# Unread TensorE products, one merged copy and a new split of work between ScalarE, GpSimd and VectorE in the first quarter of a fused attention and feed-forward kernel

## The chip, the cores and the metric

One core of a Trainium2 chip runs the kernel. Times are device microseconds (us) from the first to the last instruction of one execution, and a profile shows one execution with every engine's instructions. The engines are TensorE (PE: matmuls; PEld: its weight loads), VectorE (DVE), ScalarE (ACT), GpSimd (POOL) and SyncE (SP), which issues the transfers. Each takes its own instructions strictly in the order in which they stand in its queue.

## The reference

Attention with an additive bias that a small network makes of positions, and then two feed-forward layers over the 2304 tokens (B = 4 batches, H = 8 heads, S = 576 positions, D = 64, all float32):

```
scores = q @ k.T / sqrt(64) + bias            # bias[h,i,j] = sum_m max(x[i,j]*w1[m]+b1[m], 0) * w2[m,h]
x[i,j] = log1p(|i-j|) / log1p(max(i,1))
attn   = exp(scores - max); attn /= sum(attn) + 1e-9;  y = attn @ v
y      = (silu(y @ w_gate) * (y @ w_val)) @ w_out          # 512 -> 1536 -> 512
out    = relu(y @ w_in)**2 @ w_out2                        # 512 -> 2048 -> 512
```

The feed-forward weights come as float64, and VectorE decodes them from their bits.

## The kernel before

**Arithmetic.** Nearly every float32 product is made of three float16 ones: an operand is split into a high part and the rest (the low part), and high x high, high x low and low x high are added up. `halves` does such a split in one of several ways: 1 takes the scaled high part on GpSimd (L197) and the low part on VectorE (L191); 0 takes the high part on ScalarE (L201) and the low part on VectorE; 2 scales the whole operand in place on ScalarE (L205), rounds it there (L209), and takes the low part on GpSimd (L220). The table `MIX` gives for each kind of operand the ways that its calls take in turn; `mixed` picks the next.

**Stages.** Attention goes by query tiles of 128 rows: tile 0, 1, 2, 3 and a merged tile of the last 64 rows of each batch. Before each tile, `make_bias` makes its bias for all heads in 18 blocks of 32 keys: VectorE makes a mask (L595), TensorE multiplies it (L633), and `evac` takes the sums out of PSUM into the bias. Way 2 of `evac` has ScalarE copy both sums (L609, L615) and GpSimd multiply and add (L610, L616); way 0 has VectorE do both in two instructions that read PSUM (L612 and L618 of the changed file).

**Tile 0.** The 32 pairs of batch and head (heads, below) go one after the other. For a head, TensorE makes the scores (`scores`, L801), VectorE adds the bias and finds the maximum (L810), ScalarE takes the exponential with the row sums (L815). One head later `soft2` has TensorE transpose the float32 weights in five pieces into PSUM (L834, L835) and ScalarE copy them out (L836, L837), and `weighted` multiplies them with the values in float32 (`av`, L850). The fifth piece holds the last 64 keys. In the later tiles the weights are split into float16 halves and turned by transfers. While tile 0 runs, `prep_k` splits and transposes the keys of four heads at a time (eight groups, each with a large chunk of 512 positions and a small one of 64; the transposes are L699), and the stream of weights goes on: w_gate and w_val in thirds of 512 columns (a transfer, three decode instructions on VectorE L256 to L261, a square on ScalarE L318, a norm on TensorE L322, the split), then w_out (key "o"), whose 12 pieces are split when the scale of the whole matrix is known (L169 spreads it over the partitions).

**Feed-forward.** `moe1` takes units of 256 tokens: 24 products for each of 12 blocks (L453), a tanh on ScalarE (L461), two VectorE operations, a split, then 72 products with w_out (L476). The second layer comes at the end (L1353 and L1385).

**Order.** The program is written as generators that are taken in turn by declared costs, and a scheduler then sets the order in each engine's queue from priorities and modelled times. A change of an instruction's engine or size so moves others too. Of the 1283 us, attention and the first layer hold about the first 900, and tile 0 with its bias the first 245.

## Time and profile before

| | |
|---|---|
| median of 3 runs | 1277.08 us (1276.87 to 1277.08) |
| the profiled execution | 1284.85 us, its span 1283.2 us |
| busy: PE, DVE, ACT, POOL | 89%, 61%, 55%, 51% of the span |
| mean granted TensorE clock | 0.954 of full speed |

The share of TensorE is that of an engine that bounds most of the program. "Granted clock" is the part of TensorE's full speed that it was allowed to run at: 1.00 is 2.4 GHz and 0.50 is 1.2 GHz, and a mean between them says how long each was granted. A busy TensorE at 0.50 gets half as much done.

### The profile page before, as it was taken

To read this page: it belongs to the slowest core of one execution; us is meant where nothing else is said; L and a number is where in the kernel's file an instruction comes from. 1 tells how busy PE (TensorE), PEld (TensorE's weight loads), DVE (VectorE), ACT (ScalarE), POOL (GpSimd) and SP (SyncE) were. 2 spreads that over 40 slices of the span, in tenths; PEclk is the share of its full clock that TensorE was granted. 3 is DMA by queue.
4 is the path that set the end of the run, shared out by engine and by line. 5 is a ranking of instruction groups with operands and counts; after the bars stand their busy time and mean duration, and the time that the engine had idled before them with its cause. 6 is when DMAs were issued, how large, how long until landed. Compare 5 with 4: busy or idle time off the path is not lost.

```text
span 1283.2 us, 27543 instructions
## 1 busy us (share of the span) xinstructions
PE 1138.1 (89%) x10648; PEld 841.9 (66%) x10648; DVE 788.1 (61%) x1828; ACT 705.5 (55%) x1478; POOL 660.3 (51%) x756
## 2 busy tenths in 40 slices
PE   2568989998868999999899997989987999999998
PEld 2456768777557768687685764757436567485687
DVE  5787756788768665566573534987677352623523
ACT  5667767767657555556665432437753452715433
POOL 1851103379858666758676440324796350714423
PEclk9998678999969999999999998899999999999999
DMA  9747544127999989999789994572001010010000
GB/s 233 196 131 184 168 129 109 32 82 165 218 212 214 228 190 185 198 207 172 183 173 213 236 228 125 189 229 67 17 1 34 33 34 34 1 50 17 17 34 17
DMA packets 290110, 166.35 MB, mean 130 GB/s; under 512 B 245308, under 2 KB 258620, under 8 KB 289980
## 3 DMA queue, kind: packets, MB, share of 16 engines
q1 hardware_dynamic: 289980, 164.61, 54.9%
q8 instruction: 83, 1.36, 0.4%
q14 instruction: 47, 0.39, 0.1%
HBM read 91.60 MB, written 19.48 MB: 87 GB/s over the span
## 4 chain that ended last, share of the span: by engine, by line
PE 44%; DMA 20%; DVE 15%; POOL 8%; ACT 7%; issue 5%; SPq 1%; POOLq 0%; ACTq 0%; DVEq 0%
PE mm L1353 11%; PE mm L1385 10%; PE mm L453 8%; DMA pT<-pt 7%; PE mm L476 4%; DMA qT<-qs 3%; PE av L850 2%; POOL pt L220 2%; PE av L860 2%; DMA wr<-in_moe_w_gate_dram 2%; PE qk L801 2%; PE ma L1385 2%; POOL bias L616 2%; POOL btmp L610 2%; DMA w2s<-in_moe_w_in_dram 2%
## 5 line engine op out<-in xcount | busy, mean ns | idle before, releaser
L453 PE MATMUL mm<-xT,wr 128*128 128x256 f16 x2376 | 294.9, 281 | 11.7 <-DVE th L464 9.1
L453 PEld LDWEIGHTS <-wr 128*128 128x128 f16 x2592 | 255.3, 101 | 63.7 <-issue 21.2
L1165 POOL TENSOR_TENSOR x<-x 128x256 f32<-128x256 f32 (+1 forms) x160 | 143.5, 908 | 174.1 <-ACT x L1362 168.0
L1353 PE MATMUL mm<-wr,w2r 128*128 128x512 f16 (+1 forms) x960 | 189.9, 360 | 6.3 <-ACT x L1358 6.3
L220 POOL TENSOR_TENSOR pt<-s,pt 128x576 f16<-128x576 f32 x112 | 147.1, 1317 | 35.5 <-ACT pt L825 29.2
L1353 PEld LDWEIGHTS <-w2r 128*128 128x128 f16 x960 | 94.3, 98 | 99.2 <-issue 8.6
L220 POOL TENSOR_TENSOR z<-th,z 128x256 f16<-128x256 f32 x108 | 82.6, 765 | 138.0 <-ACT z L438 132.9
L810 DVE CUSTOM_DVE_ANT_0 s<-qk,bias 128x576 f32<-128x576 f32 x144 | 107.7, 751 | 52.6 <-PE qk L801 31.3
L476 PE MATMUL mm<-wr,z 128*128 128x512 f16 x576 | 136.0, 382 | 1.0 <-DVE th L464 1.0
L818 ACT ACTIVATE s<-s,sc 128x576 f32<-128x576 f32 x112 | 85.7, 772 | 71.5 <-DVE sc L817 63.0
L1385 PEld LDWEIGHTS <-wr 128*128 128x128 f16 x1134 | 110.6, 98 | 21.2 <-DVE wr L1165 5.6
L610 POOL TENSOR_TENSOR btmp<-btmp,xs 128x256 f32<-128x256 f32 (+1 forms) x108 | 88.2, 819 | 67.9 <-ACT btmp L609 44.3
L1165 DVE TENSOR_TENSOR wr<-x,wr 128x768 f16<-128x768 f32 (+3 forms) x60 | 78.0, 1310 | 65.6 <-ACT wr L1172 64.6
L860 PE MATMUL av<-vp,pT 128*128 128x65 f16 (+7 forms) x1920 | 87.0, 197 | 28.5 <-DMA pT<-pt 26.1
L595 DVE TENSOR_TENSOR mask<-tabT,bias 128x1024 f16<-128x1024 f16 (+1 forms) x108 | 91.7, 867 | 22.5 <-PE ma L633 16.4
L476 PEld LDWEIGHTS <-z 128*128 128x128 f16 x648 | 60.3, 98 | 66.3 <-issue 2.5
L860 PEld LDWEIGHTS <-pT 128*128 128x128 f16 (+3 forms) x1920 | 72.3, 102 | 47.7 <-DMA pT<-pt 34.4
L616 POOL TENSOR_TENSOR bias<-bias,btmp 128x256 f32<-128x256 f32 (+1 forms) x108 | 77.3, 719 | 6.1 <-DVE vp L191 0.7
L633 PEld LDWEIGHTS <-mask 128*128 128x128 f16 x1440 | 60.7, 106 | 29.9 <-issue 15.6
L1404 ACT ACTIVATE ob<-ob,fac 128x256 f32<-128x256 f32 x36 | 17.8, 506 | 105.4 <-DVE ob L1403 105.4
L462 DVE SCALAR_TENSOR_TENSOR th<-th,mm 128x256 f32<-128x256 f32 x99 | 41.0, 414 | 47.3 <-ACT th L461 45.2
L438 ACT CAST z<-th 128x256 f16<-128x256 f32 x108 | 43.0, 399 | 44.4 <-DVE th L464 43.8
(269 smaller groups left out, 2117.1 us busy)
## 6 DMA issues: line engine op xcount, KB each, us to landing
kp<-kT_d SPq DMA_DIRECT2D x64, 288.0 KB, 3.4
vp<-v_d SPq DMA_DIRECT2D x48, 325.0 KB, 4.1
w2s<-in_moe_w_in_dram SPq DMA_DIRECT2D x16, 512.0 KB, 4.2
w2s<-in_moe_w_out_dram SPq DMA_DIRECT2D x16, 512.0 KB, 4.4
wr<-in_moe_w_gate_dram SPq DMA_DIRECT2D x24, 256.0 KB, 5.0
wst<-in_moe_w_out_dram SPq DMA_DIRECT2D x12, 512.0 KB, 4.3
wr<-in_moe_w_val_dram SPq DMA_DIRECT2D x24, 256.0 KB, 4.9
v_d<-vp SPq DMA_DIRECT2D x16, 325.0 KB, 3.1
```

Of the source, the lines that this page charges most:

```text
L220: nc.gpsimd.tensor_tensor(out=out_, in0=x, in1=hi, op=ALU.subtract)
L453: nc.tensor.matmul(pg[:, 256 * gi:256 * gi + 256], wr.parts(key, f // 4, cc, wl, P * (f % 4), P), mov(xl, cc), start=k == 0, stop=k == 11)
L476: nc.tensor.matmul(po, zall[:, f, zl, P * t:P * t + P], wr.parts("o", 0, f, wl), start=k == 0, stop=k == 3 * NF1 - 1)
L595: nc.vector.tensor_tensor(out=m[:, :, ni * e:ni * e + ni], in0=block(kb, i0, ni), in1=th, op=ALU.is_gt)
L610: nc.gpsimd.tensor_tensor(out=tmp[r], in0=tmp[r], in1=xb, op=ALU.mult)
L616: nc.gpsimd.tensor_tensor(out=bias[r, :, cs], in0=bias[r, :, cs], in1=tmp[r], op=ALU.add)
L810: nc.vector.tensor_tensor_reduce(out=s.rearrange("p (a j) -> p a j", a=2), in0=pq[:, :, 0:288], in1=bias[:, n].rearrange("p (a j) -> p a j ...
L818: nc.scalar.activation(s, s, AF.Exp, bias=nm, scale=-1.0)
L860: nc.tensor.matmul(av[r, slot, 0:cn], pT[:n, 5 * l + c, r], vs[e][c][:n, c0:c0 + cn], start=m == 0, stop=m == 14)
L1165: (nc.gpsimd if how else nc.vector).tensor_tensor(out=out_, in0=a, in1=b, op=op)
L1353: nc.tensor.matmul(ph[:, :n], w2r.parts("w", g // 4, cc, wl, P * (g % 4), P), yt[:, 4 * yl + cc, :], start=m == 0, stop=m == 11)
L1385: nc.tensor.matmul(po, HS[f][:, o:o + P], st["C7"][f][wl][:, b:b + 256], start=f == 0 and k == 0, stop=f == 7 and k == 2)
```

## The change

It has five parts. (1) In tile 0, `soft2` puts four products of 128 x 512 ahead of a head's transposes; they write to the PSUM room that the transposes then overwrite, so nobody reads them. They are there as long as fewer than 14 heads have been multiplied with the values, which gives 15 heads and 60 products. (2) The fifth transpose takes the last 128 keys rather than the last 64, the values of the last 64 keys are loaded to partitions 64 to 127, and one copy of 640 columns takes the place of two. (3) `prep_k` takes way 1 for both chunks (high part on GpSimd, low part on VectorE). (4) The bias of tiles 0 and 1 takes way 2 and way 0 in turn, 9 blocks each. (5) w_out is split by way 2 (two steps on ScalarE, the rest on GpSimd) in place of way 0.

```diff
-    "g": (1, 2), "v": (1,), "o": (0,), "w": (0, 1, 2), "2": (1, 2), "K": (0, 2),
-    "V": (0,), "b": (2,), "B": (2,), "h": (0,), "H": (0, 1), "x": (0, 0, 1),
+    "g": (1, 2), "v": (1,), "o": (2,), "w": (0, 1, 2), "2": (1, 2), "K": (1,),
+    "V": (0,), "b": (2, 0), "B": (2,), "h": (0,), "H": (0, 1), "x": (0, 0, 1),
...
-                how = mixed("b" if t == 0 else "B")
+                how = mixed("b" if t in (0, 1) else "B")
...
-    def soft2(s, pt):
+    def soft2(s, pt, warm=None):
...
+            if warm is not None and av_done[0] < 14:
+
+                for _ in range(4):
+                    nc.tensor.matmul(
+                        tr[:, 0, :], ident_h, warm[:, 0:4, :], start=True, stop=True)
...
-            nc.tensor.transpose(tr[0:64, 1, 0:P], s[:, 512:S], ident)
-            nc.scalar.copy(pf[:, 0:512], tr[:, 0, :])
-            nc.scalar.copy(pf[0:64, 512:640], tr[0:64, 1, 0:P])
+
+            nc.tensor.transpose(tr[:, 1, 0:P], s[:, S - P:S], ident)
+            nc.scalar.copy(pf, tr.rearrange("p a j -> p (a j)")[:, 0:640])
...
-                n = P if c < 4 else 64
+                r = slice(0 if c < 4 else 64, P)
...
-                pT = soft2(*pend_soft[2:])
+                pT = soft2(*pend_soft[2:], st.get(("q", pend_soft[0], 0, pend_soft[1] // 4)))
```

Lines after 830 carry numbers higher by 5 to 6 in the changed file (the scores stay L801, the four transposes become L839, the fifth L841, the copy L842, the products with the values L855; the unread products are L836).

TensorE's queue about the eleventh head of tile 0, before (a name ahead of the arrow is what is written):

```order
L801 MATMUL qk<-kva,qT 128x288
L131 MATMUL mm<-ident,sc 1x128
L834 MATMUL tr<-ident,s 128x128 x4
L835 MATMUL tr<-ident,s 64x128
L850 MATMUL av<-kva,pT 128x64 x4
L801 LDWEIGHTS qT
```

and the same place in the changed kernel:

```order
L801 MATMUL qk<-kva,qT 128x288
L131 MATMUL mm<-ident,sc 1x128
L836 LDWEIGHTS ident_h
L836 MATMUL tr<-qT,ident_h 128x512
...
L855 MATMUL av<-kva,pT 128x64 x5
L801 LDWEIGHTS qT
L801 MATMUL qk<-kvb,qT 128x288
...
L839 MATMUL tr<-ident,s 128x128 x4
L841 MATMUL tr<-ident,s 128x128
```

The transposes, which wait for the exponential, have moved behind the unread products, the products with the values of an earlier head and the next head's scores.

VectorE's queue in the bias of tile 0, at its middle, before:

```order
L595 TENSOR_TENSOR mask<-tabT,bias 128x1024 x3
L256 TENSOR_SCALAR wr<-wr 128x512
L595 TENSOR_TENSOR mask<-tabT,bias 128x1024
L259 SCALAR_TENSOR_TENSOR wr<-wr 128x512
L595 TENSOR_TENSOR mask<-tabT,bias 128x1024
```

and in the changed kernel:

```order
L595 TENSOR_TENSOR mask<-tabT,bias 128x1024
L618 SCALAR_TENSOR_TENSOR bias<-qk_274,keep_207,btmp 128x8x32
L595 TENSOR_TENSOR mask<-tabT,bias 128x1024
L612 SCALAR_TENSOR_TENSOR btmp<-qk_320,keep_207,xs 128x256
L618 SCALAR_TENSOR_TENSOR bias<-qk_320,keep_207,btmp 128x8x32
L595 TENSOR_TENSOR mask<-tabT,bias 128x1024
L256 TENSOR_SCALAR wr<-wr 128x512
```

Every other block's two VectorE instructions now stand between the masks, ahead of the decodes.

ScalarE's queue at the end of tile 0, where the scale of w_out becomes known (keep_2439), in the changed kernel; before, single pieces of w_out (L201) stood here between tanh and copies:

```order
L815 ACTIVATE s,sc<-s,sc 128x576
L842 COPY pT<-tr 128x640
L735 ACTIVATE qs<-qf 128x4x2x64
L205 ACTIVATE wr<-wr,keep_2439 128x512 x12
L209 CAST wr<-wr 128x512
L461 ACTIVATE th<-mm,ux 128x256
L842 COPY pT<-tr 128x640
```

All 12 scalings stand in one block, ahead of a unit's tanh and of a head's copy. TensorE's queue there has, behind the product that spreads the scale (L169): 24 products of a unit, five transposes, 24 more products, and then the products with the values that need that copy:

```order
L169 MATMUL mm<-sc,ones_r 128x2
L453 LDWEIGHTS wr
L453 MATMUL mm<-xT,wr 128x256
...
L839 MATMUL tr<-ident,s 128x128 x4
L841 MATMUL tr<-ident,s 128x128
...
L855 MATMUL av<-kvb,pT 128x64 x5
L633 LDWEIGHTS mask
```

The products with the values (L855), which stood between the two runs of 24 before, come behind both.

## Rows read from the trace of the kernel before

**Rows 1.** Stretches: start:end, length, busy PE PEld DVE ACT POOL, clock, DMA share, GB/s
```profile
40.00:80.00 40.00, 19.72 (x251) 16.41 (x248) 32.52 (x55) 22.86 (x50) 33.24 (x33) 1.00 0.60 150
80.00:112.00 32.00, 28.69 (x234) 23.52 (x235) 27.23 (x67) 24.55 (x57) 5.02 (x6) 0.95 0.68 173
112.00:120.00 8.00, 4.82 (x29) 4.12 (x29) 4.80 (x13) 7.88 (x20) 2.23 (x2) 0.77 0.81 169
120.00:140.00 20.00, 19.16 (x91) 15.57 (x90) 16.82 (x38) 10.58 (x26) 4.73 (x4) 0.50 0.53 138
140.00:155.00 15.00, 14.02 (x84) 11.93 (x84) 10.72 (x24) 10.11 (x24) 2.76 (x3) 0.65 0.57 172
155.00:185.00 30.00, 24.22 (x160) 19.85 (x160) 14.05 (x41) 21.31 (x54) 0.66 (x1) 0.77 0.57 165
...
205.00:217.00 12.00, 11.39 (x79) 9.00 (x79) 9.44 (x26) 8.31 (x21) 4.42 (x5) 0.72 0.34 99
...
245.00:300.00 55.00, 50.91 (x627) 38.10 (x625) 42.47 (x93) 34.65 (x83) 42.26 (x50) 1.00 0.26 69
```

**Rows 2.** TensorE in order of time about 115 us: start, us, instruction, [idle before]
```profile
112.69 0.66 PE L834 MATMUL tr<-ident,s 128*128 128x128 f32 x4
...
113.98 0.27 PE L131 MATMUL mm<-ident,sc 128*1 128x128 f32 x1
117.39 1.09 PE L834 MATMUL tr<-ident,s 128*128 128x128 f32 x4 [3.13 <-DVE sc L810]
...
118.48 1.81 PE L850 MATMUL av<-kva,pT 128*128 128x64 f32 x8
```

**Rows 3.** Chain of work that ended last, 112 to 156 us: start, us, what
```profile
111.69 8.30 DMA wr<-in_moe_w_val_dram
```

**Rows 4.** The same chain over the first 82 us, shares by line
```profile
by line: DMA wr<-in_moe_w_gate_dram 24.2%; DMA wr<-in_k_dram 14.4%; issue 10.7%; POOL btmp L610 9.2%; POOL bias L616 6.8%; DMA wr<-in_v_dram 6.5%; DVE wr L256 4.5%; DVE wr L259 4.4%; DVE kvb L191 3.8%; DVE wr L261 2.9%; DVE mask L595 2.4%; 
```

**Rows 5.** Instructions of the bias of tile 0: count, ns minimum/median/maximum
```profile
L610 POOL TENSOR_TENSOR btmp<-btmp,xs x18: 716/726/5767, 22.6 to 74.5; 128x256 f32<-128x256 f32 x18
...
L616 POOL TENSOR_TENSOR bias<-bias,btmp x18: 709/784/1237, 23.5 to 75.8; 128x256 f32<-128x256 f32 x18
```

**Rows 6.** A VectorE operation of 128 x 256 that reads PSUM (line L462)
```profile
L462 DVE SCALAR_TENSOR_TENSOR th<-th,mm x18: 398/417/422, 186.5 to 296.5; 128x256 f32<-128x256 f32 x18
```

**Rows 7.** The chain in the last layer: products of 512 float16 columns
```profile
1004.43 41.44 PE mm L1353 x192
```

**Rows 8.** High part of the keys on ScalarE; a high part on GpSimd (lines L201, L197)
```profile
L201 ACT ACTIVATE kvb<-wr x7: 1041/1061/1077, 29.1 to 186.7; 128x1024 f16<-128x1024 f32 x7
...
L197 POOL TENSOR_SCALAR wr<-wr,keep x18: 695/838/1584, 64.1 to 223.4; 128x512 f16<-128x512 f32 x18
```

**Rows 9.** The two copies of tile 0 (lines L836, L837)
```profile
L836 ACT COPY pT<-tr x32: 562/572/592, 83.5 to 235.9; 128x512 f32<-128x512 f32 x32
...
L837 ACT COPY pT<-tr x32: 243/258/285, 84.0 to 237.1; 64x128 f32<-64x128 f32 x32
```

**Rows 10.** GpSimd's waits, 80 to 245 us: in total, times, longest
```profile
POOL wr L197 <- DVE keep L291: 10.4, 2, 7.9
```

**Rows 11.** The split of w_out, 232 to 262 us; GpSimd's low part (L220) earlier
```profile
L201 ACT ACTIVATE wr<-wr,keep x12: 710/722/723, 234.9 to 257.1; 128x512 f16<-128x512 f32 x12
...
L191 DVE SCALAR_TENSOR_TENSOR wr<-wr,keep x12: 740/752/1210, 235.7 to 258.2; 128x512 f16<-128x512 f32 x12
...
L220 POOL TENSOR_TENSOR wr<-wr x6: 1153/1156/1534, 69.5 to 212.7; 128x512 f16<-128x512 f32 x6
```

**Rows 12.** TensorE in order of time where w_out's scale is spread
```profile
232.15 0.38 PE L169 MATMUL mm<-sc,ones_r 1*128 1x2 f32 x2
232.46 2.79 PE L453 MATMUL mm<-xT,wr 128*128 128x256 f16 x24
...
235.81 2.78 PE L453 MATMUL mm<-xT,wr 128*128 128x256 f16 x24
```

**Rows 13.** ScalarE in order of time: two scalings in a row; first piece of w_out
```profile
62.22 1.35 ACT L205 ACTIVATE wr<-wr,keep 128x512 f32<-128x512 f32 x2
...
234.93 0.72 ACT L201 ACTIVATE wr<-wr,keep 128x512 f16<-128x512 f32 x1 [0.62 <-DVE keep L187]
```

More of the change, by code (lines that the diff above doesn't have):

```diff
@@ L650, in load_kv @@
         nc.sync.dma_start(
-            f[0:64, 1024:1280].rearrange("p (h d) -> p h d", h=4),
+            f[64 * which:64 * which + 64, 1024:1280].rearrange("p (h d) -> p h d", h=4),
             src[b, hs, 512:S, :].rearrange("h p d -> p h d"))
@@ L660, in norm_v @@
         nc.scalar.activation(
-            junk[0:64, 0:256], f[0:64, 1024:1280], AF.Square, accum_out=vss[0:64, 8 + h:9 + h])
+            junk[64:P, 0:256], f[64:P, 1024:1280], AF.Square, accum_out=vss[64:P, 8 + h:9 + h])
         x = f.rearrange("p (c d) -> p c d", d=D)
@@ L848, in weighted @@
             for c in range(5):
-                n = P if c < 4 else 64
+                r = slice(0 if c < 4 else 64, P)
                 nc.tensor.matmul(
-                    av[:, slot, 0:64], pT[:n, c, :], vs[0][c][:n], start=c == 0, stop=c == 4)
+                    av[:, slot, 0:64], pT[r, c, :], vs[0][c][r], start=c == 0, stop=c == 4)
             return
```

## The prediction, written before the result

> **What bounds the kernel now.** I cut the span into stretches first and read busy time and granted clock of each [rows 1]. Everything that the change touches lies before 300 us. From 80 to 155 us TensorE is busy for 28.69 + 4.82 + 19.16 + 14.02 = 66.7 of 75 us, so it is the bound of tile 0, yet at a clock that sinks to 0.50 (1.2 GHz). What the low clock costs in a stretch is about its busy time times one minus the clock: 1.4 us (80 to 112), 1.1 (112 to 120), 9.6 (120 to 140), 4.9 (140 to 155), 5.6 (155 to 185), 3.2 (205 to 217), 25.8 in all. Then I looked at how it begins: in order of time TensorE waits for 3.13 us at 114 us, and the four transposes that took 0.66 us take 1.09 after it [rows 2]. The chain of waits shows what was late: a transfer of w_val that lands at 120 us [rows 3], for which VectorE's decode waits ahead of a head's scores. In the stretch before, at 0.95, the same mix of scores, transposes and value products ran fast, so it can be held at the high clock, but it did not regain it by 140 us.
>
> Ahead of tile 0, from 40 to 80 us, GpSimd is busy 33.2 of 40 us and VectorE 32.5 [rows 1]. The chain over the first 82 us has GpSimd's two bias instructions with 9.2 + 6.8 = 16.0%, 13.1 us [rows 4]. After 300 us the change moves nothing by itself; the relative places of attention and feed-forward in TensorE's queue come together again there, so a gain ahead is a shift of the rest.
>
> **The change part by part.** All in us, negative is a gain.
>
> *Bias of tile 0.* Nine of 18 blocks leave GpSimd, 9 x (0.726 + 0.784) = 13.6 [rows 5]; that is half of the 13.1 on the chain, so at most -6.6. VectorE gets 18 instructions that read PSUM; the nearest row is 0.417 [rows 6], 7.5 in all. VectorE has 40 - 32.5 = 7.5 idle there [rows 1], which just covers it, so VectorE is the next bound. Without that cover the end comes 7.5 - 6.6 later: bounds -6.6 and +0.9. I take -2, since VectorE, not GpSimd, leads in the queue by then.
>
> *Unread products.* No row shows them beside float32 work. The nearest, 512 float16 columns, goes at 41.44 / 192 = 0.216 [rows 7], so 60 cost 13.0 at the high clock, 26 at the low one. They run with 15 heads, up to about 140 us. TensorE's busy time from 80 to 140 is 52.7, of which 12.1 is loss by the clock; with the products and the clock kept up it is 52.7 - 12.1 + 13.0 = 53.6. Of the 7.3 idle I leave 5, since the products fill waits for the exponential: 58.6 against 60, -1 (bounds: -6, no idle left, and +1, all of it). So up to there they only earn their price. The gain lies behind them, 140 to 155 us: if the clock is still up, TensorE needs 14.0 - 4.9 = 9.1, and VectorE with 10.7 becomes the bound of that stretch: -4 (bounds -4.3 and 0). For the two later low stretches I take 0: a wait starts them and no product stands there (bounds -8.8 and 0).
>
> On what counts as work, the trace has the heads' own mix at 0.95 up to 112 us without help [rows 1]. The Trainium skill, "TensorE: Matmul & The Clock Gate", Part 4, says that transposes do not count as busy for the clock in the way products do. By that rule the clock would drop when the products end, and the -4 would be 0; the row shows more heads held fast than the rule would let one hope, and I go by the row, with the rule as a rival.
>
> *Keys and the merged copy.* ScalarE loses eight large high parts, 8 x 1.06 = 8.5 [rows 8], and of the copies 32 x (0.572 + 0.258 - c) [rows 9]; c for 640 columns lies between 0.572 and 0.572 x 640 / 512 = 0.715, I take 0.70, which gives 4.2. ScalarE is full from 112 to 120 (7.88 of 8) and 71% busy from 155 to 185 [rows 1]; 12.7 of about 165 us is 8% of these 38, 2.9. I take -2. GpSimd's high part of 128 x 1024 is not shown: twice the row of 128 x 512 gives 1.7, its extremes 1.4 and 3.2 [rows 8], and GpSimd is nearly idle here, but the part queues behind splits that wait for a weight's scale, up to 7.9 [rows 10]. Bounds -2.9 and +5.
>
> *w_out.* Before, 12 high parts on ScalarE and 12 low parts on VectorE alternate [rows 11], hidden under products that fill TensorE, so their removal earns nothing. After, the 12 scalings stand in one block on ScalarE. Two in a row take 1.35, one 0.72 [rows 13], so 12 take 0.72 + 11 x 0.63 = 7.7. Say the scale is spread at time 0. The first piece started 2.8 later [rows 12, 13], so the block ends at 10.5, and after a rounding, a tanh and the copy, each taken as one copy of 0.57 [rows 9], a head's weights are out at 12.2. TensorE has by then 2.8 + 0.7 + 2.8 of work in front of the value products that need the copy [rows 2, 12], 6.3, and then waits 5.9. The waits in its queue that this leaves behind may cost clock as the one at 114 us did; the stretch at 0.72 cost 3.2 [rows 1]. I take +6, the wait alone; bounds 0 (the scale arrives sooner and the copy is ahead) and +16 (the clock then stays at 0.50 for 20 us of full TensorE, as from 120 to 140, a loss of 10). Queued behind the block are tanh and copies; TensorE waits for both.
>
> GpSimd gets 12 low parts, 12 x 1.156 = 13.9 [rows 11]; in that stretch it is busy 42 of 55 and loses 13.6 by the bias of tile 1, so it has room. The Trainium skill, "GPSIMD Engine Reference", § 4.1, advises VectorE for elementwise work with two inputs, GpSimd being about half as fast. The rows have 1.156 against 0.752, a ratio of 1.5; by the page's it would be 18.0 on GpSimd, which would still fit, and the sum stays.
>
> *Bias of tile 1 and the start of tile 1.* From 245 to 300 TensorE is busy 50.9 of 55 [rows 1]; at most 4.1 can be won. I take -2, bounds -4.1 and +1 (GpSimd's w_out work delays its blocks).
>
> Sum: -2 - 1 - 4 - 2 + 6 - 2 = -5. The durations come from the execution of 1284.85; it stands 7.8 above the median of 1277.08, which I take as the cost of profiling, the same for both. So 1279.9 profiled, and 1272.1, rounded 1272, as the time.
>
> **Rivals.**
> - *The clock stays up through 217 us and w_out's block hides.* For it: 35 us of low clock follow a single wait, so avoiding one may avoid several. Against: a wait of its own starts each later stretch. Another -7 of the 8.8 and -6 of the block, 1272 - 13 = 1259; with one of the two 1265.
> - *The clock falls when the products end.* With it the -4 is lost: 1276. For it: 120 to 140 us at 0.50 with the same mix; against: 80 to 112 us at 0.95. The Trainium skill's page "TensorE: Matmul & The Clock Gate", Part 4, would have it so.
> - *Slower: the block of 12 scalings decides.* Place: TensorE's value products behind it. The other terms sum to -11, so a wait and loss of clock of over 11 turns the sign; at the upper bound of +16 the sum is +5, 1282 (1280 to 1286). For it: strict queues and what followed the wait at 114 us; against: dense float16 products of a unit stand on both sides of the wait.
> - *The products do not raise the clock.* Then the 12.1 and the 4 are not won, and the half of the products that lies at the low clock pays double, +6.5: 1272 + 22.6 = 1295. Against: 2048 dense columns in a row per head are more than the scores' 4 x 288.
> - *No net change*, gains and losses of the first 300 us cancelling: 1277.
>
> **How the numbers follow.** Differences of over 0.2%, 2.6 us, can be told from none here. Chances: forecast 0.40, its own range 1267 to 1276; clock up throughout 0.20; clock falls after 0.15; the block 0.14; products without effect 0.05; no net change 0.06. Faster than 1274.5: 0.20 + nine tenths of 0.40 + a third of 0.15, 0.61. Slower than 1279.6: 0.14 + 0.05 and a little of the two near 1277, 0.22. Same 0.17. The range 1257 to 1286 leaves out the products without effect and the outer edges of the two extremes, about 0.15.
>
> **What would show it.** Right: from 120 to 140 us a clock near 1.0 and heads about 4 us apart; no more than 15 us of low clock before 217; the first scores a little before 80 us; ScalarE's 12 scalings in one run of 7.7 us with a TensorE wait of some 6 us behind it. Wrong: a clock of 0.50 beside the products; TensorE waiting on GpSimd's key parts for over 3 us; tile 0 ending later than before; a time above 1280 would mean that the block, or a new low stretch that follows it, is worse than the rows at 114 us suggest.

## The result, and the profile after

The changed kernel takes 1293.49 us (1290.62 to 1298.31; 3 runs) against 1277.08, 16 us more by these medians; the ratio on record is 1.0108 [1.0067, 1.0150], 14 us. Forecast were 1272 and a range of 1257 to 1286, so the prediction is wrong, and in direction too. A second set beside other runs of the kernel before gave 1.0082 [1.0050, 1.0114].

The profiled execution took 1293.49 us. From its page, and of its stretches those that answer to [rows 1], with the columns named there:

```profile
span 1291.5 us, 27558 instructions
PE 1147.0 (89%) x10708; PEld 845.6 (65%) x10708; DVE 782.3 (61%) x1860; ACT 686.1 (53%) x1398; POOL 654.5 (51%) x740
```

```profile
40.00:80.00 40.00, 28.74 (x295) 22.52 (x294) 37.59 (x82) 21.38 (x42) 24.78 (x18) 0.70 0.69 182
80.00:112.00 32.00, 27.36 (x234) 21.34 (x232) 25.44 (x65) 19.83 (x38) 6.70 (x7) 1.00 0.64 162
112.00:120.00 8.00, 4.57 (x30) 3.08 (x29) 5.13 (x14) 6.94 (x16) 2.96 (x2) 0.88 0.80 179
120.00:140.00 20.00, 19.00 (x119) 14.67 (x117) 17.39 (x39) 10.23 (x23) 7.10 (x7) 0.79 0.44 135
140.00:155.00 15.00, 10.53 (x71) 9.10 (x72) 10.45 (x25) 12.17 (x27) 0.40 (x1) 0.80 0.74 231
155.00:185.00 30.00, 26.30 (x167) 21.86 (x167) 11.02 (x36) 15.59 (x33) 2.19 (x3) 0.70 0.40 102
...
217.00:245.00 28.00, 24.04 (x211) 20.92 (x209) 15.19 (x47) 21.47 (x45) 9.25 (x15) 0.94 0.15 39
245.00:300.00 55.00, 47.78 (x547) 35.46 (x545) 40.98 (x98) 27.38 (x62) 35.15 (x38) 0.88 0.23 60
```

The clock is better than in [rows 1] from 80 to 155 us, as forecast, and worse from 155 to 185 and from 217 to 300. VectorE's first scores (L810) stand at 68.6 us, where they stood at 80.4, but the 17th head at 142.8 (146.5), the 32nd at 226.9 (230.5) and tile 1's first scores at 293.2 (293.1): a lead of 11.8 us is gone.

TensorE in order of time (start, us, instruction, idle before) shows what came of the two waits that the prediction dealt with, and a third:

```profile
119.06 1.87 PE L836 MATMUL tr<-qT,ident_h 128*128 128x512 f16 x4 [3.39 <-DVE sc L810]
...
126.16 1.89 PE L836 MATMUL tr<-qT,ident_h 128*128 128x512 f16 x4
...
130.68 1.03 PE L836 MATMUL tr<-qT,ident_h 128*128 128x512 f16 x4
...
240.22 1.88 PE L855 MATMUL av<-kvb,pT 128*128 128x64 f32 x10 [3.60 <-ACT pT L842]
...
273.11 1.86 PE L633 MATMUL qk<-bd,mask 128*128 128x64 f16 x32 [3.52 <-ACT bias L615]
```

The wait of [rows 2] at 114 us is still there, 3.39 us at 116, and now the unread products themselves stand behind it: the room they write in comes free only with a head's maximum on VectorE. Then they too run slowly, 1.87 us for four instead of 1.03. The second wait is that behind ScalarE's block of scalings:

```profile
231.25 7.46 ACT L205 ACTIVATE wr<-wr,keep 128x512 f32<-128x512 f32 x12 [0.56 <-DVE keep L187]
...
239.49 0.67 ACT L842 COPY pT<-tr 128x640 f32<-128x640 f32 x1
...
271.42 0.91 ACT L201 ACTIVATE vp<-wr,keep 128x256 f16<-128x256 f32 x2 [4.03 <-DMA wr<-in_v_dram]
272.24 0.45 ACT L609 ACTIVATE btmp<-qk,keep 128x256 f32<-128x256 f32 x1
272.59 0.46 ACT L615 ACTIVATE bias<-qk,keep 128x256 f32<-128x256 f32 x1
```

The block takes 7.46 us (7.7 forecast), and TensorE waits 3.60 for the copy behind it (5.9). A wait that was not forecast comes later: the values are loaded into the room of w_out's last piece, which GpSimd lets go of at 267.7 us; ScalarE waits 4.03 for that load with a bias copy queued behind it, and TensorE 3.52 for the bias.

### The profile page after: what moved, and what is told of

Same layout as the page of the kernel before. It is cut to its first block, busy times and chain, and to the rows that moved or that the text cites. A ratio compares the mean times of both kernels' runs of the same rounds, so it can differ in the third digit from the quotient of the medians.

```text
span 1291.5 us, 27558 instructions
## 1 busy us (share of the span) xinstructions
PE 1147.0 (89%) x10708; PEld 845.6 (65%) x10708; DVE 782.3 (61%) x1860; ACT 686.1 (53%) x1398; POOL 654.5 (51%) x740
## 4 chain that ended last, share of the span: by engine, by line
PE 46%; DMA 20%; DVE 16%; POOL 6%; ACT 6%; issue 4%; SPq 1%; POOLq 0%; ACTq 0%; DVEq 0%
PE mm L1358 11%; PE mm L1390 10%; PE mm L453 8%; DMA pT<-pt 6%; PE mm L476 4%; DMA qT<-qs 3%; PE av L865 2%; POOL pt L220 2%; DMA wr<-in_moe_w_gate_dram 2%; PE qk L801 2%; PE ma L1390 2%; PE av L855 2%; DVE wr L1170 2%; DMA w2s<-in_moe_w_in_dram 1%; DVE mask L595 1%
## 5 line engine op out<-in xcount | busy, mean ns | idle before, releaser
L453 PE MATMUL mm<-xT,wr 128*128 128x256 f16 x2376 | 295.9, 282 | 11.5 <-DVE th L464 6.5
L453 PEld LDWEIGHTS <-wr 128*128 128x128 f16 x2592 | 255.7, 101 | 62.3 <-issue 21.8
L220 POOL TENSOR_TENSOR pt<-s,pt 128x576 f16<-128x576 f32 x112 | 147.1, 1316 | 34.5 <-ACT pt L825 28.1
L220 POOL TENSOR_TENSOR z<-th,z 128x256 f16<-128x256 f32 x108 | 83.0, 770 | 133.6 <-ACT z L438 124.8
L810 DVE CUSTOM_DVE_ANT_0 s<-qk,bias 128x576 f32<-128x576 f32 x144 | 107.9, 750 | 59.4 <-PE qk L801 35.1
L610 POOL TENSOR_TENSOR btmp<-btmp,xs 128x256 f32<-128x256 f32 (+1 forms) x90 | 70.4, 782 | 59.8 <-ACT btmp L609 55.2
L595 DVE TENSOR_TENSOR mask<-tabT,bias 128x1024 f16<-128x1024 f16 (+1 forms) x108 | 85.7, 806 | 14.9 <-PE qk L633 7.7
L801 PE MATMUL qk<-kp,qT 128*128 128x288 f16 x384 | 66.4, 295 | 3.6 <-DMA kp<-kT_d 3.6
L1363 ACT ACTIVATE x<-mm 128x512 f32<-128x512 f32 (+1 forms) x80 | 43.1, 552 | 44.1 <-PE mm L1358 25.9
```

The costliest lines, as they stand in the source:

```text
L220: nc.gpsimd.tensor_tensor(out=out_, in0=x, in1=hi, op=ALU.subtract)
L453: nc.tensor.matmul(pg[:, 256 * gi:256 * gi + 256], wr.parts(key, f // 4, cc, wl, P * (f % 4), P), mov(xl, cc), start=k == 0, stop=k == 11)
L595: nc.vector.tensor_tensor(out=m[:, :, ni * e:ni * e + ni], in0=block(kb, i0, ni), in1=th, op=ALU.is_gt)
L610: nc.gpsimd.tensor_tensor(out=tmp[r], in0=tmp[r], in1=xb, op=ALU.mult)
L801: nc.tensor.matmul(pq[:, j, 0:288], qT[:, 2 * (n % 4) + s, :], kts[0][:, js], start=s == 0, stop=s == 1)
L810: nc.vector.tensor_tensor_reduce(out=s.rearrange("p (a j) -> p a j", a=2), in0=pq[:, :, 0:288], in1=bias[:, n].rearrange("p (a j) -> p a j ...
```

## The experiments

All but the first two rows were timed in five rounds beside the kernel before, whose runs there the ratio refers to. Head times are from VectorE's L810 in each trace, so from one execution each.

| run | median us | of the kernel before | 17th head | 32nd | tile 1's first |
|---|---|---|---|---|---|
| kernel before, first profile | 1277.08 | | 146.5 | 230.5 | 293.1 |
| changed, first profile | 1293.49 | 1.0108 [1.0067, 1.0150] | 142.8 | 226.9 | 293.2 |
| changed_again | 1292.66 | 1.0082 [1.0050, 1.0114] | 142.2 | 227.0 | 294.1 |
| before_again | 1279.31 | 0.9975 [0.9953, 0.9997] | 140.2 | 223.0 | 285.5 |
| bias_alone | 1276.82 | 0.9948 [0.9923, 0.9973] | 140.1 | 222.9 | 281.2 |
| products_alone | 1297.52 | 1.0116 [1.0086, 1.0146] | 145.6 | 237.0 | 303.3 |
| w_out_alone | 1281.91 | 1.0005 [0.9983, 1.0027] | 141.6 | 227.1 | 294.6 |
| keys_alone | 1285.48 | 1.0048 [1.0024, 1.0073] | 144.7 | 234.1 | 297.3 |
| copy_alone | 1294.52 | 1.0109 [1.0081, 1.0136] | 143.8 | 232.9 | 298.7 |
| keys_copy_alone | 1294.49 | 1.0105 [1.0083, 1.0127] | 145.9 | 232.1 | 298.0 |
| bias_copy | 1281.41 | 1.0001 [0.9983, 1.0019] | 136.0 | 223.7 | 285.8 |
| neither | 1280.78 | 1.0018 [0.9992, 1.0043] | 139.4 | 211.3 | 275.7 |
| no_products | 1276.23 | 0.9987 [0.9963, 1.0011] | 138.5 | 211.0 | 277.5 |
| w_out_back | 1278.19 | 0.9993 [0.9968, 1.0018] | 141.2 | 225.1 | 283.2 |
| products_all | 1288.57 | 1.0066 [1.0037, 1.0094] | 142.9 | 230.6 | 291.4 |
| lead_plus | 1282.61 | 0.9999 [0.9974, 1.0025] | 141.3 | 226.0 | 287.7 |
| lead_minus | 1291.13 | 1.0096 [1.0062, 1.0131] | 137.8 | 220.8 | 286.9 |
| keys_order | 1305.16 | 1.0221 [1.0178, 1.0264] | 160.4 | 248.5 | 313.1 |
| copy_redealt | 1291.58 | 1.0090 [1.0066, 1.0113] | 144.3 | 232.9 | 299.4 |
| changed_redealt | 1290.28 | 1.0092 [1.0065, 1.0118] | 142.0 | 228.1 | 287.7 |

**Undoing one part of the change.** The theory was that products and w_out's split each cost some 6 to 8 us.

```diff
# no_products
-            if warm is not None and av_done[0] < 14:
+            if False:
# w_out_back
-    "o": (2,)
+    "o": (0,)
# neither: both of these
```

> The changed kernel without the 60 unread products, all else kept. Theory A (the products cost more than they give: they stood at 68 to 110 us, where the kernel before had the clock at 1.00 too, and the lead of 11.8 us at the first scores shrank to 3.7 by the seventeenth head): about 8 us less than the changed kernel's 1293.5, so 1285, and a lead of 8 us or more over the kernel before at the seventeenth head. Theory B (the products do what the prediction took, they hold the clock and so pay for themselves): 1295 or more, with a low clock from about 100 to 145 us. Theory C (every edit deals the order anew and the end moves by up to 8 us by chance): anything between 1280 and 1300, and no relation between the head times and the end.

> The changed kernel with w_out split as before (way 0), all else kept. Theory A (the block of 12 scalings, the low parts on GpSimd alone and the load of v that waits for the last of them cost time: the lead of 3.6 us at 228 us had become a lag of 0.1 at tile 1's first scores and of 14 to 19 in the first layer's second unit): no scaling block, no TensorE wait of 3.6 behind a copy at 236, none of 3.5 for a bias at 270, no clock of 0.5 at 272 to 286; 4 to 8 us less, 1286 to 1290. Theory B (attention and first layer come together again after 300 us, so what is lost there is regained): within 2 us of 1293.5. Theory C (chance of the order): the trace at 225 to 300 mended, and the end still not where it should be.

> The changed kernel without the products and with w_out split as before; the bias, the merged copy and the keys stay changed. If products and w_out are the two losses and add up: 1293.5 - 8 - 6 = 1279, or less, since what is left (bias with a lead of 11.8 us at the first scores) is a gain: 1270 to 1279. If the lead at the first scores is lost in any case, because the weights' stream or VectorE sets the pace of tile 0: 1277 to 1285.

(The products stand at 69 to 136 us, not 68 to 110 as written there.) Either undoing alone gives back the whole loss, and both together give no more. So the loss belongs to neither part by itself: with w_out's old split the products cost nothing that can be measured (w_out_back against neither), with the new one 0.95 to 1.2%. The traces show where the two part. With the old split the products put the 32nd head 13.8 us later (w_out_back against neither), tile 1's first scores 7.5, and the 865th product of the first layer (L453) only 0.6 (457.2 against 456.6 us): the delay is made up in between, in part by the clock (from 185 to 300 us neither loses 6 us to a low one, w_out_back nothing). With the new split it stays: 15.9, 15.7 and 11.8 us (the changed kernel's first profile against no_products, 471.0 against 459.3 us at that product).

**A control that was none.** The same two ways for the keys, in the other order:

```diff
-    "K": (0, 2)
+    "K": (2, 0)
```

> The kernel before with the keys' two ways in the other order (the large chunk takes way 2, the small one way 0). A control of what a new order of the same work is worth. If order alone moves the end by several us, it differs from 1277 by over 3 us without a stretch that explains it; if not, it is 1277 within 3 us, apart from 8 large chunks that move from VectorE's low part to GpSimd's (about 8 x 1.5 us of GpSimd's idle time).

It is 2.2% slower, and a part of it is seen at once: the first scores come at 88.9 instead of 80.4 us, with the keys' large low parts moved to GpSimd, which the bias already keeps busy. By tile 1 the lag is 20 us against the first profile of the kernel before and 28 against the second. As a control of the order it says nothing; lead_plus and lead_minus below are that.

**The same programs again, and two parts alone.**

```diff
# bias_alone: the kernel before with
-    "b": (2,)
+    "b": (2, 0)
-                how = mixed("b" if t == 0 else "B")
+                how = mixed("b" if t in (0, 1) else "B")
# products_alone: the kernel before with the four unread products and the argument warm
```

> The changed kernel itself, beside the same runs of the kernel before as the others of this call, since single times of one kernel differ by several us. If the loss of 16 us is the kernel's own: 1290 to 1297. If it was drawn from the scatter: within 4 us of the kernel before.

> The kernel before itself, a second profile and a second set of times, to see how far a trace and its times scatter without any edit. Expected 1277 to 1281 as median, single times over a range of 15 to 20 us, and the places of tile 0 (first scores at 80, the 32nd head's at 231 us) within 2 us of the first profile; if those places move by more, differences of a few us between single profiles say nothing.

> The kernel before with the bias of tiles 0 and 1 in ways 2 and 0 in turn, and nothing else. Theory A (GpSimd's bias was what tile 0 waited for): first scores at 68 to 70 instead of 80 us, tile 1's first scores 10 us or more ahead, the time 4 to 8 below the kernel before. Theory B (the prediction's: VectorE is full at once, 2 us earlier): first scores at 78. Theory C (the stream of weights sets the pace of the first layer's units, so that an earlier tile 0 earns nothing): first scores at 69, the first layer's products at the same times as before up to 300 us, the time within 2 us of the kernel before.

> The kernel before with the four unread products a head in its first 15 heads, and nothing else. Theory A (they cost 60 x 0.216 = 13 us of a full TensorE, mostly where the clock was up anyway): the seventeenth head 6 to 8 us later than in the kernel before, the 32nd later by 3 or more, time 4 to 8 above the kernel before. Theory B (they keep the clock up and pay for themselves): no low clock from 116 to 150 us, the 32nd head earlier by 4 or more, time 2 to 6 below. Theory C (they only hurt together with w_out's new split): time within 2 of the kernel before.

The loss is the changed kernel's own. The second profile of the kernel before, 1275.0 us, is the most telling one of the study. Its stretches beside [rows 1], then those of products_alone:

```profile
80.00:112.00 32.00, 28.41 (x233) 23.33 (x234) 28.35 (x69) 24.47 (x56) 4.47 (x6) 0.95 0.67 175
112.00:120.00 8.00, 4.96 (x40) 3.90 (x39) 6.39 (x16) 8.00 (x21) 2.26 (x2) 1.00 0.69 163
120.00:140.00 20.00, 17.36 (x109) 14.63 (x110) 18.44 (x41) 13.05 (x31) 4.91 (x6) 0.74 0.60 167
140.00:155.00 15.00, 10.40 (x92) 8.53 (x90) 11.90 (x28) 14.15 (x39) 2.14 (x3) 0.96 0.82 252
155.00:185.00 30.00, 26.80 (x191) 22.16 (x192) 15.06 (x43) 20.01 (x47) 2.08 (x2) 0.79 0.42 125
...
205.00:217.00 12.00, 12.00 (x94) 10.19 (x92) 9.94 (x18) 6.12 (x15) 5.59 (x7) 0.85 0.48 130
```

```profile
80.00:112.00 32.00, 28.38 (x207) 20.63 (x206) 24.92 (x59) 20.11 (x46) 7.33 (x7) 0.93 0.53 132
112.00:120.00 8.00, 6.96 (x55) 5.00 (x54) 6.22 (x15) 6.78 (x15) 1.16 (x1) 0.94 0.96 242
120.00:140.00 20.00, 18.57 (x144) 14.07 (x141) 18.19 (x49) 16.09 (x40) 2.85 (x3) 1.00 0.70 212
140.00:155.00 15.00, 12.74 (x76) 9.93 (x74) 10.30 (x23) 11.54 (x31) 1.89 (x2) 0.74 0.62 191
155.00:185.00 30.00, 27.89 (x161) 22.86 (x160) 12.04 (x37) 20.11 (x48) 1.32 (x2) 0.67 0.41 116
```

The low clock from 112 to 155 us that the prediction took for the kernel's was to a good part one execution's: here 120 to 140 has 0.74 instead of 0.50 and 140 to 155 has 0.96 instead of 0.65. Busy time times one minus the clock gives 1.4 + 0 + 4.5 + 0.4 + 5.6 + 1.8 = 13.7 us of loss in the six stretches, where the first profile gave 25.8 (from 185 to 205 us, at 1.00 there, this one has 0.92, another 1.5). Against this profile the products regain, from 80 to 140 us, 5.9 - 2.4 = 3.5 us, and from 140 to 185 they lose 12.5 - 6.0 = 6.5 more. With their price of 13.0 that makes 16 us, and the time shows 15 (1.16%). But that agreement is of one pair of profiles: against the first profile of the kernel before the same sum has 9.7 regained, 2.0 lost and 5 us in all.

Profiling itself costs nothing that can be seen: in the 18 rows of the table behind the first two the profiled execution lies from 4.7 us under to 4.5 us over the median of its runs, and at it on average.

**w_out alone, the keys and the copy, and products in all heads.**

```diff
# w_out_alone: the kernel before with
-    "o": (0,)
+    "o": (2,)
# keys_copy_alone: the kernel before with "K": (1,), the fifth transpose of 128 keys, one copy, values in partitions 64 to 127
# bias_copy: bias_alone with that transpose, copy and place of the values
# products_all: w_out_back with
-            if warm is not None and av_done[0] < 14:
+            if warm is not None and av_done[0] < 99:
```

> The kernel before with w_out split by way 2, and nothing else. Theory A (the new split costs by itself: 12 scalings in a block stand ahead of the copies of the last heads, the rest waits on GpSimd, the load of v waits for the last piece and the bias of tile 1 stands behind it): a TensorE wait of 3 to 4 behind a copy after the scale, one of 3 to 4 for a bias, a low clock behind it, 8 to 14 above the kernel before. Theory B (it costs only where the products have pushed tile 0's last heads behind the block; without products it was 4 below its partner without the split): within 3 of the kernel before.

> The kernel before with the keys in way 1 and the merged copy with its fifth transpose, and nothing else. The prediction's term was -2 (bounds -2.9 and +5). If bias and these two make up the 16 us by which tile 0 ended earlier without products: 32nd head 4 or more earlier than in the kernel before, time 0 to 4 below. If GpSimd's key parts queue behind its bias work: first scores 2 or more later than 80.4.

> The kernel before with the new bias and the merged copy, keys and w_out as before, no products: the parts for which the runs so far speak. If the copy's 8 us of ScalarE count: 2 to 4 below the bias alone, so 0.6 to 0.8% below the kernel before. If they are hidden: as the bias alone, 0.2 to 0.5% below.

> The changed kernel with w_out split as before and the unread products in all heads of tile 0 but the last instead of the first 15: 16 more heads, 64 more products, 13.8 us at the high clock. If the clock falls at 147 us because the products have ended (rival of the prediction): a clock near 1.0 up to tile 0's end, some 8 us of loss regained, and the time 5 to 8 above that of the kernel with products in 15 heads (1278). If it falls by the waits of this place, whatever stands in the queue: low clock at 147 to 165 us as before, the full price, 12 to 16 above, 1290 to 1294.

w_out_alone has the block and the wait behind it. Its row among TensorE's waits from 215 to 300 us (in total, times, longest):

```profile
PE av L850 <- ACT pT L836: 3.9, 2, 3.6
```

That is the 3.6 us of the changed kernel, and yet the time is the same as without: the wait costs nothing at the end. Keys and copy, which take work off ScalarE and bring GpSimd the keys' high parts, cost 13 us. That is on the kernel before; on top of the new bias the same two cost 0.7% (neither against bias_alone), the copy 0.5% of it (bias_copy). In products_all the clock falls beside the products, so it can fall without their end:

```profile
112.00:120.00 8.00, 6.41 (x32) 5.16 (x31) 5.01 (x13) 5.79 (x14) 2.41 (x2) 0.65 0.63 147
120.00:140.00 20.00, 17.98 (x111) 14.12 (x110) 17.41 (x39) 10.26 (x22) 6.82 (x7) 0.78 0.48 141
...
155.00:185.00 30.00, 26.45 (x185) 19.95 (x185) 11.69 (x36) 16.37 (x35) 3.12 (x4) 0.83 0.39 102
```

They do soften the stretch from 155 to 185 us (0.83 where the changed kernel has 0.70), and the kernel is 0.7% slower than w_out_back for 64 products more, 9 us of a price of 13.8.

What the products do to the clock is seen best in neither and w_out_back, which differ by them alone and both come to tile 0 at a low clock. First neither, without products:

```profile
40.00:68.00 28.00, 17.02 (x227) 14.76 (x227) 26.80 (x55) 13.48 (x27) 19.18 (x15) 0.51 0.76 199
...
80.00:112.00 32.00, 23.86 (x187) 20.25 (x188) 22.83 (x61) 17.91 (x37) 6.28 (x7) 0.89 0.64 156
112.00:120.00 8.00, 8.00 (x39) 6.97 (x37) 6.37 (x15) 7.03 (x17) 3.48 (x3) 0.51 0.54 133
120.00:140.00 20.00, 16.47 (x111) 14.17 (x110) 18.75 (x44) 13.18 (x28) 8.20 (x6) 0.77 0.67 195
140.00:155.00 15.00, 10.63 (x87) 8.83 (x84) 11.01 (x27) 12.61 (x29) 3.15 (x3) 0.94 0.59 184
155.00:185.00 30.00, 27.44 (x205) 22.73 (x205) 15.52 (x44) 18.40 (x38) 2.11 (x3) 0.80 0.49 146
```

and w_out_back, whose products end at 134 us:

```profile
40.00:68.00 28.00, 17.75 (x231) 14.82 (x231) 27.42 (x55) 13.79 (x27) 15.95 (x15) 0.57 0.77 206
...
80.00:112.00 32.00, 27.10 (x231) 21.12 (x230) 25.42 (x66) 20.44 (x39) 6.79 (x7) 1.00 0.68 159
112.00:120.00 8.00, 3.54 (x26) 2.54 (x25) 4.71 (x13) 5.99 (x14) 2.41 (x2) 0.95 0.76 159
120.00:140.00 20.00, 18.07 (x132) 14.13 (x131) 19.67 (x41) 12.13 (x27) 6.60 (x7) 0.94 0.50 146
140.00:155.00 15.00, 10.99 (x66) 9.62 (x65) 9.79 (x25) 12.21 (x29) 0.40 (x1) 0.72 0.73 223
155.00:185.00 30.00, 26.11 (x181) 21.84 (x180) 12.25 (x36) 14.51 (x31) 3.66 (x4) 0.74 0.44 120
```

The clock is higher beside the products and lower behind their end. The other profiles say the same. From 155 to 185 us the five with products in 15 heads have 0.67 to 0.74, products_all has 0.83, and the partners without products (neither, no_products, the two of the kernel before) have 0.77 to 0.84. So the prediction's rival, by which the clock falls when the products end, has something for it, but their end is not the only way: copy_alone has 0.69 there without any product.

**Keys and copy apart, and the order by itself.** LEAD is a table of when the first layer takes its turn; one number of it moves no instruction to another engine.

```diff
# keys_alone: the kernel before with
-    "K": (0, 2)
+    "K": (1,)
# copy_alone: the kernel before with the transpose, the copy and the place of the values
# lead_plus, lead_minus: the kernel before with
-LEAD = [0, 39, 78, 117, 260, 400], [0, 85.669, 132.183, 165.544, 287.094, 406.094]
+LEAD = [0, 39, 78, 117, 260, 400], [0, 86.669, 132.183, 165.544, 287.094, 406.094]
+LEAD = [0, 39, 78, 117, 260, 400], [0, 84.669, 132.183, 165.544, 287.094, 406.094]
```

> The kernel before with the keys in way 1 for both chunks, and nothing else. Keys and copy together cost 1.05% (13 us) where the prediction had -2. If GpSimd's wait for the release of the keys' room (4.6 to 14.9 us seen in the traces with the new way) and the splits of weights queued behind it are the cause: 8 to 13 above the kernel before. If the copy is the cause: within 3.

> The kernel before with the merged copy, the fifth transpose of 128 keys and the values of the last 64 keys in the upper partitions, and nothing else. If the copy is the cause of the 13 us (on top of the new bias it cost 6): 5 to 13 above. If the keys are: -3 to +2. If both alone are harmless, the sum was a matter of the order that the two together deal: both within 4 of the kernel before.

> The kernel before with one number of the table by which attention and first layer take turns raised by 1 (85.669 to 86.669). No instruction changes its engine, size or number; only the order after tile 0 is dealt anew. If the order by itself is worth little: within 3 us of the kernel before. If the losses of 13 to 16 us of the single edits are to a good part those of an order that fitted the kernel before and no longer fits: 4 to 15 above.

> The same number lowered by 1 (85.669 to 84.669), again without any change to the instructions. Order worth little: within 3 us. Order decisive: 4 to 15 above, and by another amount than with the number raised.

The copy alone costs 14 us, the keys alone 6, both together 13. And an order without any changed instruction costs 0.96%, some 12 us, in one direction and nothing in the other. lead_minus loses after tile 0: its tile 1 starts in time (286.9 us).

copy_alone is ahead at the ninth head (103.1 against 105.6 us in before_again) and 8.3 us behind at the 25th (193.0 against 184.7). Its stretches there:

```profile
131.00:138.00 7.00, 5.83 (x29) 5.09 (x29) 6.64 (x17) 4.13 (x9) 1.58 (x1) 0.58 0.36 122
138.00:150.00 12.00, 10.89 (x68) 9.21 (x67) 10.41 (x22) 8.98 (x20) 3.87 (x3) 0.68 0.52 175
150.00:170.00 20.00, 15.59 (x102) 12.87 (x103) 12.20 (x37) 15.26 (x34) 0.91 (x1) 0.74 0.69 214
```

before_again has a clock of 0.83, 1.00 and 0.83 there. The lag goes with this low clock and with waits of TensorE; why they come about here is open.

**Is it the order that the edit was dealt?** Both losers with the same instructions in another order.

```diff
# copy_redealt: copy_alone, in attend
-            yield 0.5
+            yield 0.51
# changed_redealt: the changed kernel with
-LEAD = [0, 39, 78, 117, 260, 400], [0, 85.669, 132.183, 165.544, 287.094, 406.094]
+LEAD = [0, 39, 78, 117, 260, 400], [0, 84.669, 132.183, 165.544, 287.094, 406.094]
```

> The merged copy alone (14 us above the kernel before) with one declared cost of attention's generator changed from 0.5 to 0.51: the same instructions on the same engines, in another order from about the 25th head on. If the 14 us are the order that the merged copy happened to get: several us less, 1280 to 1290. If they are a wait that the copy itself brings (into tile 0's first half, which keeps its order): 1292 to 1297.

> The changed kernel with the number 85.669 lowered by 1, which stands the 12 scalings of w_out behind tile 0's last copies; the same instructions otherwise. If the block's place and the low clock behind its waits are the changed kernel's loss: no TensorE wait of 3.6 us behind a copy, 5 to 12 below the changed kernel's 1293, 1281 to 1288. If the products' 13 us of TensorE are lost whatever stands behind them: 1290 to 1296.

Both remain 0.9% slower. changed_redealt has no wait behind the block any more, and in its place another, from 215 to 300 us:

```profile
PE qk L633 <- DVE bias L618: 6.8, 5, 3.2
```

So this run alone does not decide whether the block's place is the changed kernel's loss, since other waits took the place of the one that went; against that theory stands w_out_alone, which has the same wait and loses nothing. Nor do two re-deals show that order has no part in it.

## Why the prediction was wrong, step by step

Two terms of the sum had the wrong sign, taken alone: the products (forecast -5, measured +15 on the kernel before) and keys with copy (-2, measured +13). And the sum took the terms to be independent, which the runs contradict. Why single parts and pairs cost what they do stays open in part.

- **"Loss by the low clock", 25.8 us, and the profile's time "7.8 above the median, which I take as the cost of profiling".** This is the step that failed first. A second profile of the same program has 13.7 by the same sum and took 1275.0 us, under its own median of 1279.31, and the profiles of the other kernels stand at their medians on average. So the 7.8 were not profiling but that execution, and the -4 and most of the 12.1 "regained" were to be won from a clock that the next execution did not have. That its 9.9 us more than the second profile are the clock's fits the 12.1 us more of loss, but is not shown: over 112 runs of the kernel before, the mean granted clock of a run does not go with its time (a correlation of -0.1; 1277.36 us at 0.944 beside 1284.81 at 0.963); that mean includes the stretches ahead of tile 0.
- **Unread products, -1 and -4.** Alone +15. That they raise the clock was right while they run: in the pairs that differ by them alone (w_out_back against neither, the two profiles of the changed kernel against no_products, products_alone against the two of the kernel before) 1.2 to 9.7 us less are lost to the low clock from 80 to 140 us. But from 140 to 185 us, where the -4 was to be won, 2.0 to 6.5 us more are lost. At best that leaves 7.7 of their 13.0, so up to there the clock does not pay for them in any pair. That with w_out's old split they cost nothing all the same goes with the delay being made up later, which the prediction did not have. That they "fill waits" was right for some waits only: before_again's 4.1 us of waits for the exponential (L815) from 66 to 142 us are gone in products_alone, but in the changed kernel they stand behind the same wait for a maximum. The Trainium skill's rule cited there, "TensorE: Matmul & The Clock Gate", Part 4, by which transposes do not count as busy for the clock in the way products do, fits the traces in part. From 72 to 89 us bias_alone, with float32 products, transposes and the float16 scores but no unread products, has a granted clock of 0.51, and the changed kernel with products among them 0.95; but no_products has 1.00 there without any. The prediction took from that rule that the clock falls when the products end, though a head has scores and products with the values besides its transposes. The clock is lower behind their end (above), and it fell beside them too (0.58 from 120 to 130 us), behind a wait.
- **Bias of tiles 0 and 1, -2 and -2.** The start was mis-sized: 12 us earlier, beyond the bound of -6.6, so GpSimd, not VectorE, was what tile 0 waited for (VectorE's two instructions took 0.469 and 0.472 instead of 0.417, and still fitted). Against before_again all of it is gone by the 17th head (140.1 against 140.2). There bias_alone loses 17.8 us to the low clock from 80 to 140 us and before_again 5.9; but no_products, with 5.7, keeps only 1.6 us of its 12.2, so the clock is not the whole reason. What bias_alone gains on before_again appears between the 32nd head (222.9 against 223.0) and tile 1's first scores (281.2 against 285.5). At the end it has 0.52% (6.7 us), or 0.27% if the 0.25% by which the kernel before fell below itself is taken as the measurement's error. So the sum of -4 was about right, but by luck: tile 0's half of it was won and lost again.
- **Keys and merged copy, -2, bounds -2.9 and +5.** Alone +13. The copy's duration was right (0.692, taken as 0.70). The large high part on GpSimd mostly took 1.04, not 1.7, but not always: two of the eight took 1.37 and 2.75 in the changed kernel, ahead of 70 us, and two 2.12 and 4.13 in keys_alone. Lines of the changed kernel by source line (count, ns minimum/median/maximum; that of L197 from 100 to 200 us only):

```profile
L842 ACT COPY pT<-tr x32: 669/692/699, 72.6 to 239.5; 128x640 f32<-128x640 f32 x32
L197 POOL TENSOR_SCALAR kvb<-wr x8: 397/840/1044, 99.8 to 198.4; 128x1024 f16<-128x1024 f32 x4, 64x256 f16<-64x256 f32 x4
L612 DVE SCALAR_TENSOR_TENSOR btmp<-qk,keep,xs x18: 461/469/484, 29.0 to 290.5; 128x256 f32<-128x256 f32 x18
```

  What failed was to price them by ScalarE's busy share. In copy_alone the loss comes behind the ninth head, with TensorE's waits and low clock, and its cause is not settled; another order from the 25th head on changed 3 of the 14 us, within the noise.
- **w_out, +6, bounds 0 and +16.** The mechanism was right and its parts about right (7.46 and 3.60), with a wait of 3.5 for the bias unseen. The price is not a term of its own: +0.6 alone, -4 without products (no_products against neither; their intervals overlap), 11 to 15 with them. Why the pair costs so much is not shown: without products, tile 0's last copies stand ahead of the block, and no TensorE wait over 1.9 us follows; but taking the first wait away by another order, which brought others, gained nothing.
- **"After 300 us the change moves nothing by itself".** This was wrong too. From the 865th product of the first layer (L453; 459 us in before_again, 471 in the changed kernel) to the end, the kernel before took 815 us in both profiles and the changed one 821 and 822, though no instruction there is changed; over all runs it is 812 to 825. Between 800 and 1000 us the instructions stand in another order on every engine. So some 6 of the 14 us are lost where the prediction looked at nothing. But this does not tell slow kernels from others: neither, as fast as the kernel before, took 825 us there.
- **The sum.** The parts alone add up to -0.52 + 1.16 + 1.05 + 0.05 = 1.7%; together they measure 0.8 to 1.1%, and the changed kernel without the products, or without w_out's new split, 0. Terms of 1 to 6 us were added as if the order stood still, and an order alone is worth 12, and with the bias changed the copy costs 0.5%, not 1.1. The rival that gave 1295 for products without effect on the clock came nearest in time, but not by its mechanism; the slower rival, the block, was given 1280 to 1286 and fell.

A reading that does hold over the table: where tile 1 starts by 288 us, seven of nine kernels are within 0.2% of the kernel before or faster; where it starts after 291, nine of ten (the changed kernel counted twice) are 0.5 to 2.2% slower; the first profile of the kernel before, at 293.1, was itself 7.8 us above the median. This is a reading of single profiles, not a cause. The two early exceptions are the re-dealt lead_minus and changed_redealt, the late one is w_out_alone.

## What to carry to other kernels

Take a second profile of the same program before a gain is built on the clock of a stretch, and never put the gap between a profile and the median down to profiling without one. Set the price of unread products against what the clock loses without them in several profiles: here it was 13.0 us against 7.7 at best up to 185 us. Look at the clock behind their end too, and whether they wait for the same room as the work behind them. Where a scheduler orders everything, time each part of a change alone and an order control beside them: here the bias alone is worth keeping (0.3 to 0.5%, the one version whose gain is more than that of the kernel before against itself), and none of the four others showed a gain of its own on the kernel before.

## What the runs showed of the hardware

- One program's granted clock differs between executions: 0.50 and 0.74 from 120 to 140 us. In 28 of the 29 runs of the kernel before that stood beside no_products, the time went from 1270.35 to 1285.23 us (the last took 1291.39), where the first three lay within 0.2.
- A low clock ahead of tile 0 does not delay its start. From 40 to 80 us the changed kernel's first profile has 0.70 (above), its second 1.00 at the same busy time, and the first scores come at 68.6 and 68.7:

```profile
40.00:80.00 40.00, 28.81 (x297) 22.62 (x295) 38.27 (x82) 21.43 (x42) 23.16 (x18) 1.00 0.70 183
```

- But without unread products it goes on into tile 0. Where the clock was 1.00 from 40 to 68 us, it is 0.94 to 0.98 from 80 to 112 (seven profiles without products); where it was 0.50 to 0.62, it is 0.65 to 0.89 (seven). With products it is 0.93 to 1.00 there, whatever it was before (six profiles, 0.50 to 1.00 ahead).
